# A decode attention kernel: softmax bookkeeping per half group of batches, and value products that trail the keys by 6 heads instead of 10

## The chip, the cores and the metric

The kernel runs on one core of a Trainium2 chip. The metric is the device time of the core in microseconds (us). Times are medians of several executions; most executions of one kernel here lie within 0.3% of each other, so intervals are given. A ratio in this text is the mean time of one kernel's runs over the mean of the other's runs of the same rounds, so it is not quite the ratio of the quoted medians.

## The reference

Two independent blocks A and B of cached multi-head attention for one new token, concatenated:

```python
B, Sq, D = 8, 1, 1024;  H, Sk, Dh = 32, 4096, 128         # bf16
q = (x @ wq).reshape(B, Sq, H, Dh).transpose(0, 2, 1, 3)
scores = einsum("bhqd,bhkd->bhqk", q, k_cache) * Dh ** -0.5
p = softmax(scores)
o = einsum("bhqk,bhkd->bhqd", p, v_cache)
out = o.transpose(0, 2, 1, 3).reshape(B, Sq, H * Dh) @ wo
```

There are 2 x 32 x 8 = 512 pairs of (head, batch), which this text, like the code, calls heads; each needs 1 MB of K and 1 MB of V, used once. K511 is the K load of the last head, and so on. The product of a head's exponentials with its V is called its PV. Eight heads with the same head number (the eight batches) are a group.

## The kernel before

The kernel gives each of the five engines a list of instructions; the lists meet through semaphores (`w` in the code below is what an item waits for). A slot is one head. Of the eight batches of a group, five (1, 2, 4, 5, 7) have their scores made on VectorE, three (0, 3, 6) on TensorE by transposing K. K has 6 buffers, V has 8. (The comments in the code below are added; cuts are marked by dots.)

```python
DL = cfg.get("DL", 10)            # PV of head n runs in slot n + DL
NK = cfg.get("NK", 6); NV = cfg.get("NV", 8)
...
# VectorE, per head: 4 x 8 small product-sums (the page lists x10240 and as many accumulator reads)
for jj in range(8):
    j = 8 * k + jj
    ins = d.tensor_tensor_reduce(junk[:, j, :], Kb[:, kslot, j * 128:(j + 1) * 128], q_rep[:, par, r, :],
                                 1.0, 0.0, ALU.mult, ALU.add, S2[:, par, r, j:j + 1])
...
# once a group: max on VectorE, max over partitions on GpSimd, negM on VectorE, 8 exps on ScalarE
return g.partition_all_reduce(M_sb[:, G % 2, :], m_sb[:, G % 2, :], 128, RED.max)
...
# PV of head n on TensorE waits for V and for its exp
w = [(sem_v[n % NV], 16 * (n // NV + 1)), (act_P, NB * G + b + 1)]
...
# all loads go through one queue in the order of these keys
sp_list.append((n - NK + 0.4, f"K{n}", w, sem_k[n % NK], f))            # w: K{n-6} used
sp_list.append((n - NV + DL + 0.9, f"V{n}", w, sem_v[n % NV], f))       # w: PV of n-8 done
...
sp_list.append((t, f"WQ{s}", w, sem_wq[s % 2], f))                      # 2 MB for 8 groups
sp_list.append((slot_PROJ(G) - 8, f"WO{G}", w, sem_wo[G % 2], f))       # 256 KB a group
```

Of the kernel before, what the change touches and what calls it, by code (L numbers as in the profile page):

```python
# [6 lines left out]
def bass_concat_heads__mha_block_cached__mha_block_cached__decode_kernel(  # L7
# [12 lines left out]
    cfg=None,  # L20
):
    cfg = dict(cfg or {})
    bf16, f32 = mybir.dt.bfloat16, mybir.dt.float32
    ACTF = mybir.ActivationFunctionType
    ALU = mybir.AluOpType
    AX = mybir.AxisListType
    RED = bass.bass_isa.ReduceOp
# [7 lines left out]
    NB, H, Sk, Dh = A_k_cache.shape  # L35
# [11 lines left out]
    N = NG * NB  # L47
    SCALE = float(Dh) ** -0.5

    DL = cfg.get("DL", 10)  # L50
    NK = cfg.get("NK", 6)
    NV = cfg.get("NV", 8)
    HQ = min(cfg.get("HQ", 8), H)
# [4 lines left out]
    DVB = list(cfg.get("DVB", (1, 2, 4, 5, 7)))  # L58
    PEB = [b for b in range(NB) if b not in DVB]
    NPE, NDV = len(PEB), len(DVB)  # L60
    pe_rank = {b: r for r, b in enumerate(PEB)}
    dv_rank = {b: r for r, b in enumerate(DVB)}
    T1 = cfg.get("T1", True)
    NSM = (1 if NPE else 0) + (1 if NDV else 0)
    pos = {b: r for r, b in enumerate(PEB + DVB)}
    pe_step = (PEB[1] - PEB[0]) if NPE > 1 else 1
    assert PEB == list(range(PEB[0], PEB[0] + pe_step * NPE, pe_step))[:NPE], "PE-path batches must be an arithmetic progression"

    FW = NJ * 128

    with ExitStack() as es:
# [12 lines left out]
        m_sb = E(nc.sbuf_tensor("m_sb", [128, 2, NB], f32))  # L84
        M_sb = E(nc.sbuf_tensor("M_sb", [128, 2, NB], f32))
# [27 lines left out]
        def Sp(par):  # L113
            return ps[:, 3 + par, 0:NB * NJ].rearrange("p (b j) -> p b j", b=NB)
# [42 lines left out]

        def ev_sem_cnt(Q):
            return ev_a, Q + 1

        def k_released(m):
            if is_pe(m):
# [5 lines left out]
        def add(engine, name, waits, incs, emit):  # L168
            items[engine].append((name, [w for w in waits if w is not None], incs, emit))
# [180 lines left out]
        def group_at(i, off):  # L350
            if i >= off and (i - off) % NB == 0 and (i - off) // NB < NG:
                return (i - off) // NB
            return None
# [14 lines left out]

        def exp_item(G, b):
            par = G % 2  # L370
            w = []
            if b == 0:
                w.append((dve_nm, G + 1))
                if G < 2:
                    w.append((dve_init, 1))
                else:
                    w.append((pe_pv, NB * (G - 2) + NB))
                    w.append((pool_L, G - 1))
            if b in pe_rank:
                src = Sp(par)[:, b, :]  # L380
            else:
                src = S2[:, par, dv_rank[b], :]

            def f(a, G=G, b=b, par=par, src=src):
                return a.activation(Ppad[:, par, b, :, b, :], src.rearrange("p (c m) -> p c m", m=4),  # L385
                                    ACTF.Exp, bias=negM[:, par, pos[b]:pos[b] + 1], scale=SCALE,
                                    accum_out=l_sb[:, par, b:b + 1])
            add("act", f"EXP{G}.{b}", w, [(act_P, 1)], f)

        def dqk_item(n, k):  # L390
            G, b, blk, h = head_info(n)
            par = G % 2
            r = dv_rank[b]
            kslot = n % NK
            w = []
            if k == 0:
                w.append((sem_k[kslot], 16 * (n // NK + 1)))
                w.append(dve_done(("QR", (G, len(QRCH) - 1))))
                if v_idx(n) >= 1:
                    w.append((dve_qk, v_idx(n)))  # L400
                if r == 0 and G >= 2:
                    w.append((sm_m, NSM * (G - 1)))
                    w.append((act_P, NB * (G - 2) + NB))

            def f(d, par=par, r=r, kslot=kslot, k=k):
                ins = None
# [4 lines that stand above are left out]
                return ins  # L411
            add("dve", f"DQK{n}.{k}", w, [(dve_qk, 1)] if k == 3 else [], f)
# [79 lines left out]
        for i in range(NSLOT):  # L492
# [18 lines left out]
            if 1 <= i <= N and is_pe(i - 1):  # L511
                n = i - 1
                e = e_idx(n)
                G, b, blk, h = head_info(n)
                for q in range(NQ):
                    w = []
                    if q == 0:
                        w.append(dve_done(("QP", G)) if T1 else dve_done(("QS", G // HQ)))
                        if pe_rank[b] == 0 and G >= 2:
                            w.append((sm_m, NSM * (G - 1)))  # L520
                            w.append((act_P, NB * (G - 2) + NB))
                    w.append(ev_sem_cnt(NQ * e + q))
                    add("pe", f"QK{n}.{q}", w, [(pe_qk, 1)] if q == NQ - 1 else [], emit_QK(n, q))
            if DL <= i < N + DL:
# [32 lines left out]
            if i == 0:  # L557
                for blk in range(NBLK):
                    w = [rd_burst_wait(("XT", blk))]

                    def f(d, blk=blk):
                        return cp(d, xT[:, blk, :], Mp_b[:, 0:CC * NB])
                    add(COPY_ENG, f"XTC{blk}", w, [(dve_mp, 1)], f)
            Gx = group_at(i, NB + 1)
            pe_head = i < N and is_pe(i)
            if pe_head:
                evac_item(i, 0)
                evac_item(i, 1)
            if Gx is not None:
                for b in range(0, NB // 2):  # L570
                    exp_item(Gx, b)
            if pe_head:
                evac_item(i, 2)
                evac_item(i, 3)
            if Gx is not None:
                for b in range(NB // 2, NB):
                    exp_item(Gx, b)
            if COPY_ENG == "act":
                G = group_at(i, NB - 1 + DL)
                if G is not None:  # L580
# [27 lines left out]
                    return d.tensor_copy(ident_f[:], ident[:])  # L608
                add("dve", "init_idf", [(s_id, 1), (dve_init, 4)], [(s_hm, 1)], f)
            dv_head = i < N and not is_pe(i)  # L610
            G = group_at(i, NB)
            if G is not None:
                par = G % 2
                if NPE:
                    w = [(pe_qk, NPE * (G + 1))]
                    if G >= 2:
                        w.append((pool_M, G - 1))

                    def f(d, G=G, par=par):
                        return d.tensor_reduce(m_sb[:, par, 0:NPE],  # L620
                                               Sp(par)[:, PEB[0]:PEB[0] + pe_step * (NPE - 1) + 1:pe_step, :], AX.X, ALU.max)
                    add("dve", f"MAXA{G}", w, [(sm_m, 1)], f)
                if NDV:
                    w = [(dve_qk, NDV * (G + 1))]
                    if G >= 2:
                        w.append((pool_M, G - 1))

                    def f(d, G=G, par=par):
                        return d.tensor_reduce(m_sb[:, par, NPE:NB], S2[:, par, :, :], AX.X, ALU.max)  # L629
                    add("dve", f"MAXB{G}", w, [(sm_m, 1)], f)  # L630
            G = group_at(i, NB + 2)
            if G is not None:
                w = [(pool_L, G + 1)]
                if G >= 2:
                    w.append(dve_done(("OEX", G - 2)))

                def f(d, G=G):
                    return d.reciprocal(rL[:, G % 2, :], L_sb[:, G % 2, :])
                add("dve", f"RCP{G}", w, [(dve_rl, 1)], f)
            if dv_head:  # L640
                dqk_item(i, 0)
            burst_reads(i, "dve")
            if dv_head:
                dqk_item(i, 1)
            G = group_at(i, NB)
            if G is not None:
                w = [(pool_M, G + 1)]
                if G >= 2:
                    w.append((act_P, NB * (G - 2) + NB))

                def f(d, G=G):
                    return d.tensor_scalar_mul(out=negM[:, G % 2, :], in0=M_sb[:, G % 2, :], scalar1=-SCALE)  # L652
                add("dve", f"NEGM{G}", w, [(dve_nm, 1)], f)
            if dv_head:
                dqk_item(i, 2)
            G = group_at(i, NB - 1 + DL)
# [30 lines left out]
            return g.affine_select(ident[:], ones[:], [[1, 128]], ALU.is_equal, 0.0, base=0, channel_multiplier=-1)  # L687
        add("pool", "ident", [(s_pl, 5)], [(s_id, 1)], f)
        for G in range(NG):
            w = [(sm_m, NSM * (G + 1))]  # L690
            if G >= 2:
                w.append((dve_nm, G - 1))

            def f(g, G=G):
                return g.partition_all_reduce(M_sb[:, G % 2, :], m_sb[:, G % 2, :], 128, RED.max)  # L695
            add("pool", f"PMAX{G}", w, [(pool_M, 1)], f)
            w = [(act_P, NB * G + NB)]
            if G >= 2:
                w.append((dve_rl, G - 1))

            def f(g, G=G):
                return g.partition_all_reduce(L_sb[:, G % 2, :], l_sb[:, G % 2, :], 128, RED.add)
            add("pool", f"PADD{G}", w, [(pool_L, 1)], f)

        sp_list = []
        for blk in range(NBLK):
# [129 lines left out]
```

## Time and profile before

| | before |
|---|---|
| time | 2826.86 us median of 15 (2822.33 to 2833.12) |
| span of the first profiled execution | 2831.6 us (that was the slowest of the 15) |
| span of a second profiled execution, taken later | 2825.4 us |
| read from memory | 1107.33 MB |

The first lines are the page's part 1 (busy time of each engine, share of the span, instructions) and part 3 (DMA queues: packets, bytes, share of 16 engines' span) of the kernel before:

```profile
PE 1922.3 (68%) x15328; PEld 1226.3 (43%) x15328; DVE 2272.0 (80%) x20935; ACT 684.3 (24%) x1997; POOL 51.5 (2%) x138
...
q1 hardware_dynamic: 165056, 1107.43, 96.3%
q8 instruction: 124, 2.03, 0.3%
q14 instruction: 204, 1.67, 0.1%
HBM read 1107.33 MB, written 0.03 MB: 391 GB/s over the span
```

No compute engine is full; the DMA engines are 97% busy. PE is TensorE's matmuls, PEld its weight loads, DVE is VectorE, ACT ScalarE, POOL GpSimd. The page gives queues 8 and 14 the kind "instruction"; in the trace the packets of queue 8 have 16384 bytes and those of queue 14, but for a few small ones, 8192.

The next view cuts the trace of the kernel before into windows. The columns are the window, its length, each engine's busy time, the granted clock of TensorE, the mean busy share of the 16 DMA engines, and GB/s:

```profile
10.00:25.00 15.00, 12.00 (x169) 11.50 (x170) 4.67 (x43) 5.85 (x13) 0.89 (x3) 0.84 1.03 423
25.00:40.00 15.00, 0.74 (x22) 0.57 (x19) 14.65 (x139) 0.32 (x1) 0.00 (x0) 0.50 0.60 217
40.00:60.00 20.00, 12.21 (x107) 10.11 (x108) 19.09 (x177) 7.96 (x26) 0.76 (x2) 0.59 1.01 421
980.00:984.00 4.00, 4.00 (x33) 1.73 (x33) 0.23 (x4) 0.99 (x2) 0.00 (x0) 0.66 1.01 399
984.00:988.00 4.00, 4.00 (x40) 1.97 (x37) 4.00 (x38) 0.00 (x0) 0.00 (x0) 1.00 0.83 313
988.00:992.00 4.00, 0.29 (x3) 0.12 (x2) 3.83 (x37) 0.00 (x0) 0.00 (x0) 1.00 0.11 40
992.00:996.00 4.00, 2.17 (x12) 1.95 (x13) 4.00 (x38) 1.19 (x3) 0.00 (x0) 0.62 0.06 27
996.00:1000.00 4.00, 4.00 (x16) 2.46 (x15) 3.83 (x37) 2.00 (x4) 0.00 (x0) 0.53 0.98 299
```

Two holes are to be seen: one at the start, and one of 8 us, right after a wq load, in which the share falls to 0.06, that is one DMA engine of 16 (1/16 is 0.0625; from 990.43 to 996.29 us the packet records show 8 KB packets of 0.31 us one after the other, each starting as the last ends). Elsewhere the rate stands at some 420 GB/s for long stretches. The queue of SyncE in that second hole, in order of time (start, length, what was issued), shows that nothing else is issued meanwhile: the K issue after the wq load takes 15.72 us to go through, and the next V issue starts at 995.85.

```profile
975.06 2.15 SPq L729 DMA_DIRECT2D wq_sb<-in_A_wq_dram  x1
980.09 15.72 SPq L715 DMA_DIRECT2D Kb<-in_A_k_cache_dram  x1
995.85 1.42 SPq L720 DMA_DIRECT2D Vb<-in_A_v_cache_dram  x1
```

The end of the kernel before, from the timeline of TensorE: the last PVs run one by one as V lands.

```profile
2812.82 7.08 PE L269 MATMUL ps<-Vb,Ppad 128*32 128x512 bf16 x32
2820.32 1.90 PE L269 MATMUL ps<-Vb,Ppad 128*32 128x512 bf16 x8 [0.42 <-DMA Vb<-in_B_v_cache_dram]
2822.79 1.90 PE L269 MATMUL ps<-Vb,Ppad 128*32 128x512 bf16 x8 [0.57 <-DMA Vb<-in_B_v_cache_dram]
```

### The profile page before, as it was taken

The page shows a single profiled execution, that of the slowest core. Times are in us where ns is not written, and L with a number is a line of the kernel's source. Part 1 is how long each engine was busy: PE and PEld are TensorE (multiplying, and loading weights), DVE is VectorE, ACT ScalarE, POOL GpSimd, SP SyncE. Part 2 cuts the span into 40 slices and gives each one's busy share as a digit, 9 for nine tenths or more (in the row PEclk, how much of TensorE's full clock was granted, in tenths as well). Part 3 has the DMA queues.
Part 4 walks back from the last instruction along what each step waited for, and adds up shares of the span by engine and source line. Part 5 has one row for each costly group of instructions (what it writes and reads, how often), then busy time and mean ns, then how long its engine had stood idle before and what let it go on. Part 6 is the DMA issues. An engine that isn't in the chain of part 4 may idle for free.

```text
span 2831.6 us, 58099 instructions
## 1 busy us (share of the span) xinstructions
PE 1922.3 (68%) x15328; PEld 1226.3 (43%) x15328; DVE 2272.0 (80%) x20935; ACT 684.3 (24%) x1997; POOL 51.5 (2%) x138
## 2 busy tenths in 40 slices
PE   4677666766667676666766666667667766676677
PEld 3444434444444444444444444444444444444443
DVE  7987788877888778888788887878878788787885
ACT  2222222222122222222222222222222222222222
POOL 0000000000000000000000000000000000000000
PEclk7878788887888887888878888788787887788878
DMA  8999999999999999999999989999899998999996
GB/s 354 420 419 418 374 416 402 391 387 373 414 401 388 386 382 420 402 393 365 394 419 403 394 352 405 419 402 397 340 415 419 410 393 348 420 417 393 399 390 261
DMA packets 165384, 1111.13 MB, mean 392 GB/s; under 512 B 17568, under 2 KB 17568, under 8 KB 33984
## 3 DMA queue, kind: packets, MB, share of 16 engines
q1 hardware_dynamic: 165056, 1107.43, 96.3%
q8 instruction: 124, 2.03, 0.3%
q14 instruction: 204, 1.67, 0.1%
HBM read 1107.33 MB, written 0.03 MB: 391 GB/s over the span
## 4 chain that ended last, share of the span: by engine, by line
DMA 52%; DVE 31%; PE 14%; issue 1%; SPq 1%; ACT 0%; DVEq 0%; POOL 0%; POOLq 0%
DVE junk L409 29%; DMA Kb<-in_B_k_cache_dram 28%; DMA Kb<-in_A_k_cache_dram 24%; PE ps L229 8%; PE ps L269 5%; DVE S L409 1%; DMA Vb<-in_B_v_cache_dram 1%; SPq L720 1%; PE ps L332 1%; SPq L715 1%; PE ps L312 0%; SPq L737 0%; DVE Qe L453 0%; ACT q_rep L417 0%; DVE acc L476 0%
## 5 line engine op out<-in xcount | busy, mean ns | idle before, releaser
L409 DVE CUSTOM_DVE_ANT_0 junk<-Kb,q_rep 128x128 bf16<-128x128 bf16 x10240 | 2211.6, 286 | 322.8 <-DMA Kb<-in_B_k_cache_dram 156.5
L269 PE MATMUL ps<-Vb,Ppad 128*32 128x512 bf16 x4096 | 1013.9, 398 | 5.1 <-ACT Ppad L385 3.0
L229 PE MATMUL ps<-ident_f,Kb 128*128 128x128 f32 x3072 | 619.0, 385 | 508.5 <-DMA Kb<-in_B_k_cache_dram 268.4
L409 DVE DVE_READ_ACCUMULATOR2_ANT S<- 128x1 f32 x10240 | 838.8, 82 | 0.1
L229 PEld LDWEIGHTS ps<-ident_f,Kb 128*128 128x128 f32 x3072 | 552.1, 204 | 549.2 <-DMA Kb<-in_B_k_cache_dram 287.6
L366 ACT COPY KT<-ps 128x512 f32<-128x512 f32 x768 | 435.7, 589 | 1192.6 <-PE ps L229 1192.0
L269 PEld LDWEIGHTS ps<-Vb,Ppad 128*32 128x32 bf16 x4096 | 380.8, 100 | 505.7 <-issue 143.5
L312 PE MATMUL ps<-ident,q_all 128*128 128x128 bf16 x320 | 54.1, 292 | 375.0 <-DVE Qe L453 326.0
L417 ACT CAST q_rep<-ps 128x512 bf16<-128x512 f32 (+1 forms) x128 | 54.4, 425 | 789.5 <-PE ps L312 789.5
L312 PEld LDWEIGHTS ps<-ident,q_all 128*128 128x128 bf16 x320 | 28.7, 121 | 394.3 <-DVE Qe L453 330.1
L250 PEld LDWEIGHTS ps<-Qe,KT 128*128 128x128 bf16 x6144 | 167.8, 97 | 54.1 <-issue 53.5
L250 PE MATMUL ps<-Qe,KT 128*128 128x2 bf16 x6144 | 182.8, 163 | 0.2
L476 DVE TENSOR_TENSOR acc<-ps,acc 128x64 f32<-128x64 f32 x62 | 13.9, 225 | 164.2 <-PE ps L332 164.2
L385 ACT ACTIVATE Ppad<-S,negM 128x32 bf16<-128x32 f32 x320 | 100.0, 318 | 0.0
L323 PEld LDWEIGHTS ps<-Sel,Dg_sb 32*128 32x128 f32 x512 | 61.6, 186 | 28.8 <-issue 26.6
L323 PE MATMUL ps<-Sel,Dg_sb 32*128 32x8 f32 x512 | 67.2, 253 | 4.0 <-ACT q_all L417 2.8
L695 POOL PARTITION_ALL_REDUCE M_sb<-m_sb x64 | 23.4, 366 | 2489.3 <-DVE m_sb L629 2489.3
L385 ACT ACTIVATION_READ_ACCUMULATOR Ppad<-S,negM 128x1 f32 x320 | 63.4, 198 | 0.0
L586 ACT COPY Dg_sb<-ps 32x512 f32<-32x512 f32 x64 | 36.7, 574 | 103.3 <-PE ps L269 103.3
L385 ACT ACTIVATE Ppad<-ps,negM 128x32 bf16<-128x32 f32 x192 | 54.5, 284 | 19.8 <-DVE negM L652 19.8
L385 ACT ACTIVATION_READ_ACCUMULATOR Ppad<-ps,negM 128x1 f32 x192 | 38.6, 201 | 0.0
L652 DVE TENSOR_SCALAR negM<-M_sb 128x8 f32<-128x8 f32 x64 | 11.0, 172 | 31.6 <-POOL M_sb L695 31.6
(36 smaller groups left out, 198.6 us busy)
## 6 DMA issues: line engine op xcount, KB each, us to landing
Kb<-in_A_k_cache_dram SPq DMA_DIRECT2D x256, 1024.0 KB, 24.8
Vb<-in_A_v_cache_dram SPq DMA_DIRECT2D x256, 1024.0 KB, 26.7
Kb<-in_B_k_cache_dram SPq DMA_DIRECT2D x256, 1024.0 KB, 25.0
Vb<-in_B_v_cache_dram SPq DMA_DIRECT2D x256, 1024.0 KB, 26.8
wq_sb<-in_A_wq_dram SPq DMA_DIRECT2D x4, 2048.0 KB, 33.1
wo_sb<-in_A_wo_dram SPq DMA_DIRECT2D x32, 256.0 KB, 25.5
wq_sb<-in_B_wq_dram SPq DMA_DIRECT2D x4, 2048.0 KB, 33.3
wo_sb<-in_B_wo_dram SPq DMA_DIRECT2D x32, 256.0 KB, 25.6
```

The costliest lines, as they stand in the source:

```text
L229: ins = pe.transpose(dst[:, tt * 128:(tt + 1) * 128], kf[:, t * 128:(t + 1) * 128], ident_f[:])
L250: ins = pe.matmul(S[:, c:c + 2], lhsT=ktb[:, t * 256 + e:(t + 1) * 256:2], rhs=Qe[:, G % 2, pe_rank[b], e, :], start=(e == 0), stop=(e == 1))
L269: ins = pe.matmul(Dg(par), lhsT=Ppad[:, par, b, c].rearrange("p a m -> p (a m)"), rhs=Vb[:, vslot, c * 512:(c + 1) * 512], start=(b == 0 a ...
L312: ins = pe.matmul(Mp_f[:, r * 128:(r + 1) * 128], lhsT=q_all[:, G, b:b + 1].broadcast_to([128, 128]), rhs=ident[:], start=True, stop=True)
L323: ins = pe.matmul(Mp_f[:, 0:NB], lhsT=Dg_sb[0:32, par, jj * 128:(jj + 1) * 128], rhs=Sel[0:32, jj, :], start=(jj == 0), stop=(jj == 3))
L332: ins = pe.matmul(Mp_f[:, c * NB:(c + 1) * NB], lhsT=wo_sb[:, G % 2, c * 128:(c + 1) * 128], rhs=oT[:, G % 2, :], start=True, stop=True)
L366: return a.copy(dst, src)
L385: return a.activation(Ppad[:, par, b, :, b, :], src.rearrange("p (c m) -> p c m", m=4), ACTF.Exp, bias=negM[:, par, pos[b]:pos[b] + 1], sc ...
L409: ins = d.tensor_tensor_reduce(junk[:, j, :], Kb[:, kslot, j * 128:(j + 1) * 128], q_rep[:, par, r, :], 1.0, 0.0, ALU.mult, ALU.add, S2[:, ...
L417: return eng.copy(dst, src) if COPY_ENG == "act" else eng.tensor_copy(dst, src)
L586: return a.copy(Dg_sb[:, G % 2, :], Dg(G % 2))
L715: return sp.dma_start(Kb[:, n % NK, :], Ks[blk][b, h].rearrange("(p j) d -> p (j d)", p=128))
```

## The change

The intent is to finish the softmax of the first four batches of a group without waiting for the other four, so that exps and PV come earlier, and PV can trail the scores by 6 heads instead of 10. Max, all-reduces and negM are done once per unit of four batches; V's places in the load queue move four heads ahead with DL.

```diff
-    DL = cfg.get("DL", 10)
+    DL = cfg.get("DL", 6)
...
+    UNITS = [list(u) for u in cfg.get("UNITS", ((0, 1, 2, 3), (4, 5, 6, 7)))]
...
-            if b == 0:
-                w.append((dve_nm, G + 1))
+            if b == UNITS[ui][0]:
+                w.append((dve_nm, U + 1))
...
-            Gx = group_at(i, NB + 1)
...
-            if Gx is not None:
-                for b in range(0, NB // 2):
-                    exp_item(Gx, b)
+            for ui in range(NU):
+                Gx = group_at(i, UNITS[ui][-1] + 2)
+                if Gx is not None:
+                    for b in UNITS[ui]:
+                        exp_item(Gx, b)
...
-            G = group_at(i, NB)          # MAXA, MAXB, NEGM once a group
+            def max_items(i):            # MAXA, MAXB per unit
+                for ui in range(NU):
+                    G = group_at(i, UNITS[ui][-1] + 1)
+            def negm_items(i):           # NEGM per unit
...
-            def f(g, G=G):
-                return g.partition_all_reduce(M_sb[:, G % 2, :], m_sb[:, G % 2, :], 128, RED.max)
+                def f(g, par=par, p0=p0, nb_u=nb_u):
+                    return g.partition_all_reduce(M_sb[:, par, p0:p0 + nb_u], m_sb[:, par, p0:p0 + nb_u], 128, RED.max)
```

(Cut: the semaphore counts that follow from it, the sum all-reduce, done alike.)

## The prediction

> **What bounds the kernel now.** The page counts the 16 DMA engines busy for 96.7% of the span (96.3 + 0.3 + 0.1), 391 GB/s read; VectorE is 80% busy, TensorE 68%, ScalarE 24%. The chain of waits is 52% K loads, 31% VectorE products. In 2-us windows, long stretches run at 420 GB/s; at that rate 1107 MB take 2637 us (an estimate). The other 190 us, from the same windows:
> - 25 to 40 us: DMA share 0.60, about 6 us lost. V loads queue behind K8, which waits for VectorE to free K2.
> - About every 350 us (8 groups), seven times, right after a 2 MB wq load: some 8 us at a share of 0.06, one engine of 16, while the next K issue sits 15.7 us. Together about 60 us.
> - Shallow dips later in each period, 70 to 80 us in all.
> - The end: share 0.06 in 2795-2800 and 2815-2825.

> A share of 0.06 is one lagging engine. Why one may lag: queue 8 (instruction) moves 2.03 MB in 124 packets, 127 us if one engine carries them. [...] Per engine, data packets of 8 KB (median 0.31 us) and 2 KB (0.085 us) come to some 2650 us; plus 127 us and the edges is near 2800. So I read the middle as bound by the slowest DMA engine [...], not by softmax latency.

> **What the change does.** Softmax bookkeeping goes per half group (four batches); PV trails K by 6 heads, not 10. Added per group: one max over PSUM (0.25 us now), one over S2 (0.31), one negM (0.17), two all-reduces on GpSimd (0.37 each). At half size, about 0.5 us of VectorE per group, some 30 us over 64 groups, on an engine idle 20%. Bytes, matmuls, exps, buffers (6 K, 8 V) and K order are unchanged. V moves four slots earlier in the queue, but its buffer comes free four slots earlier too: same prefetch depth.

> **On the critical path.** Middle: about 0. The stall after wq stays; VectorE's waits for the all-reduce are 32 us in all, off the bound.
> Start: V0 and V1 go ahead of K6, V2 ahead of K7; first PV near 46 us instead of 57.6. The 25-40 us hole should close: 5 to 7 us.
> End: today eight PVs (2 us each) remain after the last group's exps (2806.8), and V loads wait for buffers. After: four PVs remain, and the hole at 2795-2800 closes. But the lagging engine fills that hole today, so I count 3 to 6 us.

> **Prediction: 2818 us**, 8 in 10 between 2799 and 2834. Faster by over 2%: 4%. Within 2%: 94%. Slower by over 2%: 2%.

> **What would show it.** Right: DMA share from 25 to 40 us near 1.0; first PV before 50 us; the stalls after wq remain at one-engine share; mean GB/s near 393; VectorE busy up 20 to 35 us without the span; last exp to end shrinks from 25 us to under 20. Wrong: if stalls or dips shrink (above 400 GB/s, under 2790 us), V order or the eight-head release of buffers limited the DMA, not one engine. If VectorE's waits for PROJ or max on PE exceed 300 us, K is released late and time rises.

> **What would make it wrong.** Earlier V loads may shift the phase in which wq fills the queue; a V issue waiting on a PV in the common queue could block K issues behind it.

(Two passages are cut from the prediction that no trace of this case shows; they were offered in support of reading queue 8 as instructions fetched by one engine, and of the DMA bound. No term of its sum is cut: 2650 us of data packets, 127 us and the edges, near 2800. The 127 us are the time of queue 8's 124 packets of 16384 bytes in the trace, 1.03 us each; that one engine carries them was the author's assumption.)

## The result, and the profile after

| | before | after |
|---|---|---|
| time, median | 2826.86 us (15 runs) | 2839.99 us (12 runs, 2833.95 to 2846.34) |
| ratio | | 1.0043, 95% interval 1.0032 to 1.0055 |

The change made the kernel 0.43% slower, where 9 us faster was predicted. It counts as the same within 2%, but 2840 lies outside the stated range of 2799 to 2834. The same parts of the page, of the changed kernel:

```profile
PE 1904.3 (67%) x15328; PEld 1206.1 (42%) x15328; DVE 2298.2 (81%) x21127; ACT 686.0 (24%) x1997; POOL 108.4 (4%) x266
...
q1 hardware_dynamic: 165056, 1107.43, 96.3%
q8 instruction: 124, 2.03, 0.3%
q14 instruction: 209, 1.71, 0.2%
HBM read 1107.33 MB, written 0.03 MB: 390 GB/s over the span
```

VectorE gained 192 counted instructions and 26 us, as foreseen, and queue 14 five packets. The page's chain of waits is of no help here: in the changed kernel it ends in 93% "issue", so it lost the trail. The windows of the changed kernel:

```profile
10.00:25.00 15.00, 12.85 (x185) 12.20 (x185) 5.28 (x47) 6.17 (x13) 0.09 (x1) 1.00 1.02 422
25.00:40.00 15.00, 0.12 (x5) 0.02 (x1) 14.65 (x138) 1.25 (x8) 1.07 (x2) 0.58 1.01 420
40.00:60.00 20.00, 15.58 (x137) 10.22 (x138) 19.16 (x179) 6.44 (x18) 0.85 (x3) 0.80 1.02 422
996.00:1000.00 4.00, 0.85 (x5) 0.45 (x5) 4.00 (x40) 0.85 (x2) 0.00 (x0) 0.60 0.17 68
1000.00:1004.00 4.00, 3.76 (x18) 3.40 (x19) 2.71 (x26) 1.89 (x4) 0.00 (x0) 0.55 0.07 29
1004.00:1008.00 4.00, 4.00 (x51) 2.71 (x50) 0.99 (x8) 0.45 (x1) 0.00 (x0) 1.00 0.74 261
```

The hole at the start is gone (share 1.01 from 25 to 40 us), so 6 us were won there; yet the hole of the third wq load after the start now comes some 8 us later than before. Much of that is order alone: four more V loads and one more wo load now stand ahead of this wq load in the queue, 10.6 us by the bare times of the ledger below, of which the 6 us won are to be taken off. Only some 4 us were lost on the way to there. The end, again from TensorE's timeline:

```profile
2817.32 3.63 PE L290 MATMUL ps<-Vb,Ppad 128*32 128x512 bf16 x16
2824.30 7.07 PE L290 MATMUL ps<-Vb,Ppad 128*32 128x512 bf16 x32 [3.35 <-ACT Ppad L408]
```

TensorE waits 3.35 us for the last four exps and then runs four PVs after them, where the kernel before had one PV left when its last V landed.

### A ledger of the lagging engine

In the trace every K and V load has 16 increments of its semaphore, each with a time. In the kernel before the 16th comes 15.3 us (median over K loads) after the 15th and 17.8 us after the first, while the first 15 come within 1.9 us of each other (median). I read an increment as the landing of one DMA engine's share of the load. Times fit: a 1 MB load has 128 packets of 8 KB, a sixteenth of them is 8, and 8 of 0.31 us make 2.48 us, the interval found below; in the hole of 988 to 996 us eight 8 KB packets run between two packets of 4 bytes, at 992.28 and 994.74 us, and there are 17568 of those, 16 for each of 1098 loads. So one share in sixteen lags, by 8 us or more in 93% of the K loads (95% from 60 us on). The increments do not name their engine; that each is an engine's, and the 16th the same one's throughout, is inferred, from the even intervals below and from the holes in which one engine works alone. Taken so, the last increments of successive loads, in order of the queue, are a log of that one engine. From that log (landings of the trace, worked out, not a view of the profile):

- From 100 us on, the interval between two last increments has a median of 2.48 us for 1 MB loads in which no instruction packet starts (711 intervals of the kernel before), also 2.48 us if a queue-8 packet starts in it (94 intervals), and 3.45 us if one queue-14 packet does (158 intervals, of which 31 are no longer than 3.1 us, so not every queue-14 packet lengthens them). So a queue-14 packet that falls on this engine costs it 0.97 us (3.45 less 2.48), and a queue-8 packet nothing. I call these packets fetches, reading them as instructions on their way to an engine: queue 14 gained 20 packets with 2560 instructions more (pad_dve, pad_pool) and lost 150 with 19200 fewer (mulred), below.
- In a hole after wq, where only this engine works, the packet records show it directly (start, end in us, queue, bytes; a 4-byte packet at 636.829 is left out):

```
636.212 636.521 q1 8192
636.518 636.842 q14 8192
636.841 637.797 q1 8192      <- 0.96 us instead of 0.31
637.794 638.109 q1 8192
```

Taking 2.486 us for each K or V load (the median interval of the run mulred below), 5.44 for wq (64 packets of 2 KB at 0.085 us) and 0.68 for wo (8 of them) as the bare time of its shares (together 2632.7 us), the ledger of this engine is:

| us beyond the bare time | before, 2nd trace | changed, 1st | changed, 2nd |
|---|---|---|---|
| to 50 us (start) | 12.2 | 6.4 | 7.0 |
| 50 us to its last landing (middle) | 172.3 | 186.5 | 184.4 |
| last landing to the end | 8.2 | 12.6 | 12.3 |
| bare time and these: the span | 2825.4 | 2838.2 | 2836.4 |
| of the middle (counted from 60 us): K and V intervals with a fetch, over 3.1 us | 162, 157.9 us | 167, 160.9 us | 164, 158.6 us |
| of the middle: seven wq loads | 11.2 | 21.4 | 19.0 |
| of the middle: all else | 2.3 | 3.3 | 5.9 |

The first trace of before was its slowest execution; its middle is 178.2, its wq loads 16.4, so beside it the change's middle is only 6 to 8 us longer. With the second, which is near the median, the change comes to -5.5 us at the start, +13.2 in the middle and +4.2 at the end (means of the two changed traces), in sum +11.9; the timed difference was 13 us.

### The profile page after: what moved, and what is told of

The parts are those of the page before. It is cut to its first block, busy times and chain, and to the rows that moved or that the text cites. A ratio compares the mean times of both kernels' runs of the same rounds, so it can differ in the third digit from the quotient of the medians.

```text
span 2838.2 us, 58793 instructions
## 1 busy us (share of the span) xinstructions
PE 1904.3 (67%) x15328; PEld 1206.1 (42%) x15328; DVE 2298.2 (81%) x21127; ACT 686.0 (24%) x1997; POOL 108.4 (4%) x266
## 2 busy tenths in 40 slices
DMA packets 165389, 1111.18 MB, mean 392 GB/s; under 512 B 17568, under 2 KB 17568, under 8 KB 33984
## 3 DMA queue, kind: packets, MB, share of 16 engines
q1 hardware_dynamic: 165056, 1107.43, 96.3%
q8 instruction: 124, 2.03, 0.3%
## 4 chain that ended last, share of the span: by engine, by line
issue 93%; POOL 4%; DVE 2%; PE 1%; POOLq 0%; ACT 0%; DVEq 0%
DVE junk L431 2%; POOL L_sb L744 2%; POOL M_sb L737 2%; PE ps L290 0%; PE ps L250 0%; POOLq L797 0%; DVE S L431 0%; PE ps L344 0%; PE ps L333 0%; PE ps L313 0%; ACT q_rep L439 0%; PE ps L300 0%; ACT o_sb L439 0%; PE ps L271 0%; PE ps L353 0%
## 5 line engine op out<-in xcount | busy, mean ns | idle before, releaser
L250 PE MATMUL ps<-ident_f,Kb 128*128 128x128 f32 x3072 | 599.3, 376 | 551.0 <-DMA Kb<-in_B_k_cache_dram 288.4
L250 PEld LDWEIGHTS ps<-ident_f,Kb 128*128 128x128 f32 x3072 | 534.8, 199 | 594.1 <-DMA Kb<-in_B_k_cache_dram 308.7
L485 DVE TENSOR_TENSOR oT<-ps,rL 128x8 bf16<-128x8 f32 x64 | 10.7, 167 | 227.3 <-PE ps L344 227.3
L737 POOL PARTITION_ALL_REDUCE M_sb<-m_sb x128 | 47.6, 372 | 2380.2 <-DVE m_sb L658 2380.2
L744 POOL PARTITION_ALL_REDUCE L_sb<-l_sb x128 | 59.3, 463 | 328.4 <-ACT Ppad L408 328.4
L674 DVE TENSOR_SCALAR negM<-M_sb 128x4 f32<-128x4 f32 x128 | 21.1, 165 | 31.8 <-POOL M_sb L737 31.8
```

The costliest lines, as they stand in the source:

```text
L250: ins = pe.transpose(dst[:, tt * 128:(tt + 1) * 128], kf[:, t * 128:(t + 1) * 128], ident_f[:])
L674: return d.tensor_scalar_mul(out=negM[:, par, p0:p0 + nb_u], in0=M_sb[:, par, p0:p0 + nb_u], scalar1=-SCALE)
L737: return g.partition_all_reduce(M_sb[:, par, p0:p0 + nb_u], m_sb[:, par, p0:p0 + nb_u], 128, RED.max)
L744: return g.partition_all_reduce(L_sb[:, par, b0:b0 + nb_u], l_sb[:, par, b0:b0 + nb_u], 128, RED.add)
```

## The experiments

Theory A: one DMA engine, which besides its sixteenth of the loads also fetches VectorE's instructions, paces the program from end to end; the change costs where it adds to that engine, and at the end. Rival B: the shorter PV lag and the new order of K and V loads cost the middle. Rival C: what counts is VectorE's or GpSimd's own work. All runs were correct, 4 to 6 runs each, against the kernel before on the same chip.

### split_dl10: only the split

```diff
-    DL = cfg.get("DL", 6)
+    DL = cfg.get("DL", 10)        # in the changed kernel
```

> The changed kernel with its PV lag set back to 10 heads, so that only the split of the softmax into half groups is left. Theory A (one lagging DMA engine, which also fetches VectorE's instructions, paces the program; the split costs its added instructions there, about 3 to 5 fetches of 0.97 us each): 2 to 8 us over before, no gain at the start (share 0.6 between 25 and 40 us again), last V landing to end back to about 9 us. Theory B (the loss in the middle comes from the shorter PV lag and the V loads that now go ahead of K): the middle is as fast as before, time within 2 us of before.

Measured: 2829.33 us median, ratio 1.0014 (1.0001 to 1.0026), that is 4 us over before; share 0.66 between 25 and 40 us; last V landing to the end 8.8 us. The split alone costs about what its 378 more VectorE instructions should: by the run below, 22.7 us for 2560 instructions, an estimate of 3.3 us. The trace taken (2835.37 us) is 6 us over the run's median. The interval reaches down to 0.3 us, and the medians differ by 0.8, so it may cost next to nothing. Most of the loss came with the lag of 6, so B is not out by this run.

### pad_dve and pad_pool: instructions alone

```diff
+                for c in range(8):      # pad_dve: in each of VectorE's 320 heads
+                    add("dve", f"PAD{i}.{c}", [], [], lambda d, c=c, r=v_idx(i) % 2: d.memset(padv[0:1, r, c:c + 1], 0.0))
```
```diff
+            for c in range(40):         # pad_pool: after each group's sum all-reduce
+                add("pool", f"PAD{G}.{c}", [], [], lambda g, c=c, r=G % 2: g.memset(padv[0:1, r, c:c + 1], 0.0))
```

> The kernel before with 2560 one-element memsets added to VectorE, 8 in each of its 320 heads; 20 more instruction fetches of 8 KB. Theory A: each adds 0.97 us on the lagging engine, so 17 to 22 us longer (about 2847), though VectorE had 20% idle; the intervals of 3.45 us between last increments go up by 20. Rival (VectorE's slack hides its own added work, fetches cost nothing): 0 to 3 us.

> The kernel before with 2560 one-element memsets added to GpSimd, 40 after each sum all-reduce; also 20 more fetches of 8 KB. Theory A with GpSimd's fetches on another DMA engine: within 3 us of before. If they fall on the lagging engine too: 17 to 22 us longer. Rival of A (any added instruction traffic costs all): same as the VectorE padding.

Measured: pad_dve 2850.12 us, ratio 1.0080 (1.0066 to 1.0094), so 22.7 us longer. pad_pool 2827.2 us, ratio 1.0002 (0.9989 to 1.0016). Both pads are 2560 one-element memsets and 20 more packets of 8192 bytes on queue 14, one for each 128 instructions added. The page of pad_dve, parts 1 and 3:

```profile
PE 1912.1 (67%) x15328; PEld 1219.6 (43%) x15328; DVE 2307.1 (81%) x23495; ACT 684.4 (24%) x1997; POOL 52.7 (2%) x138
...
q14 instruction: 224, 1.84, 0.2%
```

and the same parts of the page of pad_pool:

```profile
PE 1919.7 (68%) x15328; PEld 1221.9 (43%) x15328; DVE 2271.8 (80%) x20935; ACT 683.2 (24%) x1997; POOL 119.5 (4%) x2698
...
q14 instruction: 224, 1.84, 0.2%
```

VectorE was busy only 35 us more in a span with over 500 us of idle time, and the time still grew by 22.7 us, just over what A expected; the log of the lagging engine has 178 long intervals among K and V instead of 161 or 162, so 16 or 17 more where 20 were expected. The same packets for GpSimd cost nothing. A expects this: the fetches that cost are VectorE's. That GpSimd's land on another DMA engine is inferred, since the records do not name the engine. C is not out by these two runs: VectorE's work is on part of the chain that ended last (31% of it in the kernel before), so 35 us more of it could cost time by themselves. The run mulred, below, decides that.

### skip15: take shares off one DMA engine

```diff
-            sp_list.append((n - NV + DL + 0.9, f"V{n}", w, sem_v[n % NV], f))
+            for x, (pa, pb) in enumerate(((0, 120), (120, 128)) if n % 8 == 7 else ((0, 128),)):
+                # loads Vb[pa:pb, ...] from rows pa:pb; the PV's wait counts both
+                sp_list.append((n - NV + DL + 0.9 + 0.001 * x, f"V{n}.{x}", w if x == 0 else [], sem_v[n % NV], f))
```

> The kernel before with every eighth V load issued as two loads, of 120 and of 8 partitions[...]. Theory A: [...]it sheds 64 shares of 2.48 us (159 us) and the time falls to 2690 to 2760 us, where the others bound[...]. Rival (the middle is bound by waits between engines of the core or by HBM): within 5 us of before.

(The diff is shortened. "It" in theory A is the lagging engine. 2690 to 2760 us was the forecast if the split spared it, and otherwise no change or some 20 us more.)

Measured: 3214.65 us, ratio 1.1376, 386 us longer. Every expectation missed. The trace has 16 + 9 increments for a pair of split loads, where one whole load has 16, and the page 448 more small packets (18016 against 17568 under 512 B), 7 for each of the 64 pairs. The 8 KB packets became slower: of 8 KB packets, 10880 took between 0.5 and 0.7 us, against 685 in the kernel before, and one engine still lagged, by 19.5 us. Why such a split slows packets was not tried further, and which of the 16 the lagging engine is stays open.

### dv4 and mulred: fewer VectorE instructions

```diff
-    DVB = list(cfg.get("DVB", (1, 2, 4, 5, 7)))
+    DVB = list(cfg.get("DVB", (1, 3, 5, 7)))     # dv4: TensorE takes a fourth head of each group
```
```diff
-                for jj in range(8):               # mulred
-                    j = 8 * k + jj
-                    ins = d.tensor_tensor_reduce(junk[:, j, :], ..., S2[:, par, r, j:j + 1])
+                j0 = 16 * (k // 2)
+                if k % 2 == 0:
+                    return d.tensor_tensor(junk[:, j0:j0 + 16, :], <16 K rows>, <q_rep broadcast>, ALU.mult)
+                return d.tensor_reduce(S2[:, par, r, j0:j0 + 16], junk[:, j0:j0 + 16, :], AX.X, ALU.add)
```

> The kernel before with four instead of five of eight heads on VectorE (TensorE takes the fifth). 4096 fewer VectorE instructions, 32 fewer fetches. Theory A (lagging DMA engine with VectorE's fetches): 25 to 35 us faster, about 2797, although TensorE gets 64 heads of 4.6 us more. Rival (memory traffic or waits bound the middle, fetches matter only as bytes): within 5 us of before; or slower if TensorE binds.

> The kernel before with VectorE's 64 small instructions of a head (32 product-sums, each with an accumulator read) replaced by 4 large ones (two products of 128x2048, two sums), for about the same VectorE time (an estimate: 7 us a head, as now). Some 19000 fewer VectorE instructions, about 150 fewer fetches. Theory A: the 17-us lag of one engine goes, 100 to 150 us faster, 2680 to 2730 us, the DMA then even. Rival: within 10 us of before, or slower if the large instructions take longer.

(The 4.6 us of TensorE a head agree with 3.67 us for a head's 16 transposes and 0.94 for its 32 score products from 1026.52 us on in the first trace of before. 7 us a head is VectorE's 2272.0 us over its 320 heads; that the large instructions would take as long was the guess, and no run had shown it.)

(The diff of mulred is shortened; a semaphore between product and sum is left out.) Measured: dv4 2789.65 us, ratio 0.9871 (0.9855 to 0.9887), 37 us faster. mulred 2679.97 us, ratio 0.9487 (0.9471 to 0.9502), 147 us faster. The long intervals of K and V fell from 161 to 129 in dv4, just the 32 fetches saved. The page of dv4, parts 1 and 3, also tells whose instructions queue 8 carries:

```profile
PE 2088.5 (75%) x18336; PEld 1344.8 (48%) x18336; DVE 1840.7 (66%) x16839; ACT 794.9 (28%) x2189; POOL 53.2 (2%) x138
...
q8 instruction: 148, 2.42, 0.4%
q14 instruction: 175, 1.43, 0.1%
```

```profile
PE 1908.8 (71%) x15328; PEld 1210.8 (45%) x15328; DVE 2276.9 (85%) x1735; ACT 685.4 (26%) x1997; POOL 73.8 (3%) x138
...
q8 instruction: 124, 2.03, 0.3%
q14 instruction: 54, 0.44, 0.0%
HBM read 1107.33 MB, written 0.03 MB: 414 GB/s over the span
...
L412 DVE TENSOR_REDUCE S<-junk 128x16 f32<-128x2048 bf16 x640 | 1463.1, 2286 | 17.6
L409 DVE TENSOR_TENSOR junk<-Kb,q_rep 128x2048 bf16<-128x2048 bf16 x640 | 780.8, 1220 | 180.9 <-DMA Kb<-in_B_k_cache_dram 71.2
```

VectorE is as busy as before (2277 against 2272 us) and has 1735 instructions instead of 20935; the bytes loaded are the same. The large differences are 19200 fewer VectorE instructions and, with them, 150 fewer instruction packets; the core reads at 414 instead of 391 GB/s. (The trace is of the fastest of the five executions, 2676.35 us.) The lag of the 16th increment falls from 15.3 to 0.2 us (median), and the hole after wq is gone; this window of mulred holds the third wq load's landings:

```profile
944.00:948.00 4.00, 4.00 (x46) 1.95 (x44) 3.97 (x3) 0.00 (x0) 0.00 (x0) 0.99 1.01 392
948.00:952.00 4.00, 0.06 (x1) 0.00 (x0) 3.00 (x5) 0.00 (x0) 0.37 (x1) 0.87 1.04 421
```

So theory A holds for what bounds the kernel, and C does not: with VectorE as busy as before, the time fell by 147 us. (For the same 2048 columns the product took 1220 ns and the sum 2286 ns.)

### after_again and tail_k: the changed kernel once more, and its end

```diff
-            sp_list.append((n - NV + DL + 0.9, f"V{n}", w, sem_v[n % NV], f))
+            sp_list.append((n - NV + (10 if n >= N - 12 else DL) + 0.9, f"V{n}", w, sem_v[n % NV], f))   # tail_k
```

> The changed kernel once more, for a second trace and the spread of one. Ratio to before 1.003 to 1.006; last V landing to the end again near 13 us (before 9); the middle (K64 landed to K448 landed) again 5 to 11 us over before's 2109.9. If the middle comes out within 2 us of before, the first trace's middle was spread.

> The changed kernel with the last 12 V loads put back to the queue places they had before, so that the last K loads go ahead of them. Theory (the change's tail is lost because four more V loads stand ahead of the last K, so the last head's VectorE work, exps and four PVs come after the last byte): K511 lands some 10 us earlier relative to the end, last V landing to end back from 13.3 to about 9 us, 3 to 6 us faster than the changed kernel of the same rounds. Rival (the tail is set by the end of the lagging engine whatever the order): within 2 us of it.

Measured: after_again 2843.11 us, ratio 1.0055 (1.0042 to 1.0068); its middle from K64 to K448 took 2115.0 us against 2109.9, at the low edge of what was expected. tail_k 2834.68 us, ratio 1.0033 (1.0017 to 1.0049), 6 us (0.22%) under after_again; the two intervals overlap a little. In its trace K511 lands at 2795.8 instead of 2810.1 us, but VectorE, with earlier heads still to do, ends only at 2815.9 instead of 2820.9; so the last V landing to the end shrank from 13.3 and 12.9 us only to 12.2, not to 9. The rest of its gain is an earlier last V, which also holds spread of the middle. So it is not shown that the order of the last loads makes the change's end: with K511 landed 14 us earlier the end stayed nearly as long, and what came last was VectorE's backlog.

### before_again, after_mulred, after_mulred_tailk: the change where no engine lags

> The kernel before against itself, for a second trace. Ratio 0.998 to 1.002. The first trace of before fell on its slowest execution (2833 of a median of 2827), so here the lagging engine's excess over its bare data time after 60 us should be 167 to 175 us, below the first trace's 177; then the middle of the changed kernel costs it 8 to 14 us more than before, not the 6 to 8 that the first traces show.

> The changed kernel with VectorE's 64 small instructions of a head replaced by 4 large ones, as in the run that did this to the kernel before (2680 us). Theory: the change costs in the middle because it adds to the lagging engine; without that lag the middle costs nothing, and what is left is the start (5 to 6 us won) and the end (4 us lost): 2675 to 2683 us, within 4 us of that run. Rival (the change costs the middle through its shorter PV lag or the split itself): 8 us or more over that run, 2688 or more.

> The same with the last 12 V loads in the queue places of the kernel before. Theory: start kept, end mended, 2668 to 2677 us, 3 to 6 us under the run without this; the fastest of all. Rival as above: no better than 2680.

(The last two put the edit of mulred, and those of mulred and tail_k, on the changed kernel; before_again has no edit.) Measured: before_again 2826.65 us, ratio 0.9998 (0.9984 to 1.0012); its excess after 60 us is 171.4 us, and the changed kernel's 185.6 and 183.5, so 12 to 14 us more, as expected. after_mulred 2676.66 us, ratio 0.9467 (0.9452 to 0.9481). after_mulred_tailk 2676.24 us, ratio 0.9469 (0.9453 to 0.9484), 0.4 us under the run without it where 3 to 6 were expected: the end was not mended; a miss.

With the small instructions the change costs 0.43 to 0.55%; with the large ones, where no engine lags, its ratio to before is 0.9467 against mulred's 0.9487, the same within the intervals, if anything faster (each is measured against before in its own rounds, on different chips). The ledger's middle (50 us to the last landing) is 20.8 us with the change and 22.0 without. The edges do move, and cancel: the start is 5.4 instead of 11.7 us, the last landing to the end 15.9 instead of 8.2. So neither the lag of 6 heads nor the order of V and K costs the middle by itself; against B, the middle's cost was there only while one DMA engine lagged. In after_mulred_tailk K511 lands at 2637.4 instead of 2646.0 us, but VectorE ends its last head's sums at 2656.4 instead of 2657.2: it is 86% busy, and its work, not the load of K511, comes last there.

### mulred_start: only the early V loads

```diff
-            sp_list.append((n - NV + DL + 0.9, f"V{n}", w, sem_v[n % NV], f))
+            sp_list.append((n - NV + (6 if n < 4 else DL) + 0.9, f"V{n}", w, sem_v[n % NV], f))   # on mulred
```

> The kernel before with the 4 large VectorE instructions a head (2680 us), and of the change only this: the first four V loads four places earlier in the queue. Theory: the DMA hole between 25 and 40 us closes and the end stays as before (about 8 us from last V landing): 5 to 7 us under the run without it, 2672 to 2676 us, a little under the whole change on top of the large instructions (2677). Rival (the hole at the start is made up later): 2679 to 2681.

Measured: 2679.29 us, ratio 0.9482 (0.9469 to 0.9495): no gain that shows, as the rival said. The hole between 25 and 40 us closed, but another opened (windows of mulred_start):

```profile
25.00:40.00 15.00, 0.00 (x0) 0.00 (x0) 14.60 (x9) 0.00 (x0) 0.00 (x0) 0.50 1.02 423
40.00:50.00 10.00, 6.59 (x60) 6.22 (x61) 9.66 (x8) 3.45 (x7) 0.00 (x0) 0.50 0.73 281
```

Moving four V loads closes one hole and opens a smaller one later; the changed kernel has none in this place, with all its V loads ahead and its first PV at 48.3 instead of 57.6 us. The second hole is worth only 2.7 us, though. By the ledger the start to 50 us is 6.1 us shorter than in mulred and the middle 8.3 us longer (30.3 against 22.0), nearly all of it at the last wq loads (7.7 against -0.4). As mulred's trace is 3.6 us under its median, part of this is spread. It shows no more than that moving the first four loads is not enough.

## Why the prediction was wrong

- "So I read the middle as bound by the slowest DMA engine": right, and settled by pad_dve, dv4 and mulred (22.7 us longer, 37 and 147 us shorter).
- "queue 8 (instruction) moves 2.03 MB in 124 packets, 127 us if one engine carries them": wrong queue; by dv4 (24 packets more with 3008 matmuls and as many weight loads more) it carries TensorE's instructions. A queue-8 packet does not lengthen the lagging engine's interval (2.48 us with and without). It is queue 14, at 0.97 us a packet, for VectorE's share of its packets, some 157 us of the middle. That the sum came near the measured time was luck. The packets of queue 14 take only 0.32 us themselves; in the list above the rest of the 0.97 lies in the data packet behind, which the page books under queue 1.
- "Middle: about 0": this step failed. The middle came out 12 to 14 us longer than in the second trace of before. The step looked only at VectorE's idle time. But VectorE's 20% of idle time does not make 378 more VectorE instructions (semaphore waits counted) free when the DMA engine that paces the program fetches them; pad_dve puts them at 3.3 us (an estimate), and the log's fetch intervals show 1 to 3 us. A larger part, 8 to 10 us between the traces compared, is the seven wq loads, which took this engine longer; why they did stays open (next point).
- The wq term is unsteady: 11.2, 16.4 and 14.8 us in the three traces of before and pad_pool, 11.6 in pad_dve, 16.4 in split_dl10, 21.4 and 19.0 in the two of the change, but 15.1 in tail_k, which has the change's order in all but its last loads. Without the lag it is mostly small (-0.4 in mulred, 0.7 and 1.4 with the change on it), but 7.7 in mulred_start. The packet records tell what most of it is. A 2 KB packet takes 0.084 us (median), but of the lagging engine's wq packets, once the 15 others have their wq share, 75 and 82 of some 408 took over 0.15 us in the two traces of the change; all of them together come to 16 us over that median. A rougher count for the other traces, in which packets of a wo load had to be set aside, gives 10.5 and 5.2 us in those of before, 12.4 in pad_pool and 11.3 in tail_k. Fetches do not explain the growth: in five of the seven intervals of the change no queue-14 packet starts. Whether and how the change makes more wq packets slow was not tested. The prediction had named "the phase in which wq fills the queue" among what would make it wrong, and put no number on it; the trace shows the K issue of 15.72 us after a wq load, not whether a queue is full.
- "End: [...] so I count 3 to 6 us": this failed in sign, +4.2 us. V loads four heads further ahead put four more MB in front of the last K, which the prediction did not count. K511 landed at 2810 to 2812 us instead of 2793 to 2799, and exps and four PVs then followed the last V. That this order alone is the cause is not shown, since tail_k, which moved K511 back, left 12.2 us. The sign given for it ("last exp to end shrinks from 25 us to under 20") came true, from 22.5 to 13 us, and meant nothing: the last exp itself had moved later.
- "Start: [...] 5 to 7 us": right, 5.5 us, and most of the other signs named (share near 1.0, first PV before 50 us, one-engine stalls after wq, VectorE busy up 26 us) came true as well. They were signs of what I had thought of, and did not look at the terms that I had set to zero. The one that did, a mean rate near 393 GB/s, up from 391, failed: it was 390.
- "Bytes, matmuls, exps, buffers and K order are unchanged": true of the counts, but K's place against V was not unchanged, and the end came out longer.

## What to carry to other kernels

When the DMA engines are busy nearly throughout, as here (97%), compare the 15th with the 16th semaphore increment of the loads (here 15.3 us apart, 0.2 in mulred): if one engine lags, look at what it does besides the loads, here the instruction stream of the engine with 20000 small instructions, and make that stream shorter. Replacing 64 small VectorE instructions a head by 4 large ones, at equal VectorE time, gained 5%, where a restructured softmax lost 0.4%. Judge a change of load order at its ends: loads moved ahead put others behind, here the last K by four V loads, and what is still to be done when the last byte has landed can grow (by 4 us here, by 8 on top of mulred).
